# Attention and state-space kernel on one core: small loads reordered, an interleaving moved from GpSimd to VectorE, the last block's stores moved to SyncE, planner durations edited

## The chip, the cores and the metric

The kernel runs on one core of a Trainium2 chip. A core has five engines, each with its own instruction queue that is worked off in order: TensorE (PE in the profile; PEld are its weight loads), VectorE (DVE), ScalarE (ACT), GpSimd (POOL) and SyncE (SP). SP and ACT, and POOL in another way, also issue DMAs. The metric is device time in microseconds of one execution; it is compared as the median of several.

## The reference, cut to what matters

One sequence of 2048 rows and 448 columns goes through two branches that are mixed by a gate per row.

```
g = sigmoid((x * gate_w).sum(-1))
# A: 16 query heads of width 28, one shared key and value head
q = x @ wq;  k = x @ wk;  v = x @ wv
a = softmax(q k^T / sqrt(28)) v  @ wo
# B: a diagonal state-space model with 256 complex modes for each of 448 channels
dt = exp(log_dt);  K[d,l] = Re sum_n C[d,n] dt[d] B[d,n] exp(dt[d] A[d,n] l)
b = causal_convolution(K, x) + x * Dskip
out = g * a + (1 - g) * b
```

The scores are 16 heads x 2048 x 2048 exponentials. The convolution has one filter K of 2048 taps for every channel; the kernel makes the taps from tables of powers and convolves with matmuls on Toeplitz slices of the taps.

## The kernel before, in words

**Attention.** The scores are 1024 tiles of 128 keys by 512 queries (16 groups of a query chunk and four heads, 64 tiles each). TensorE makes a tile into one of five PSUM banks (lines 1289 and 1312, and 1300 and 1303 for the last 64 tiles), ScalarE exponentiates sets of three and two tiles in turn (line 1344, 410 instructions), and TensorE multiplies each with V (lines 1362 and 1356). Q of a later group is projected on TensorE (line 857), its absolute values and its copy are taken by VectorE (lines 863 and 869), and a copy in another layout, qM, is made by DMAs from POOL.

**Head.** Four x tiles are loaded by SP, transposed by TensorE (line 639), and copied by ScalarE (line 649) or VectorE (line 653) to xT. From them come K (line 661, copied by line 673), its maxima (line 668), V and the gate (line 684). The step sizes dt are spread over partitions by a matmul (line 768) and exponentiated by ScalarE (line 770). The raw parameters are transposed (line 781) and multiplied on VectorE (line 792); sines come from ScalarE (lines 798 and 799), whose table for the sine is loaded at a dummy instruction of one element (line 678) and whose table for the exponential is loaded again at another (line 800). Lines 804 and 807 are six more exponentials on 128x896, `tab` and five powers `mq`. K's and V's weights and `log_dt` are loaded by ACT's DMA queue, the rest by SP's.

**Convolution.** The channels are 14 blocks of 32. For each, VectorE builds the tables of powers (lines 896 to 916, 936 to 986; line 986 is the last of a block), TensorE multiplies them to taps (line 1009, 64 matmuls a block), VectorE copies the taps (line 1019), and POOL's DMAs write them to a scratch in device memory (KP_scratch). SP's DMAs load them back shifted, as slices T (some land in the buffer of U). Two convolutions of 16 channels each (128 matmuls each on line 1071, with x interleaved as U) follow, each with a product on VectorE (line 1080), a reversal by TensorE (line 1091) and an addition into O (line 1100). U is made from x rows in O by 16 copies on POOL (line 598) into U and T, and spread by SP's DMAs.

**End.** Three of four query chunks go through the output projection (line 1109) and are folded into O on VectorE (line 1118). The last chunk is normalised by matmuls (lines 1171 and 1178) and VectorE (1374, 1182, 1184), its four row tiles add O by a matmul with the identity (line 1209) and the projection (line 1205), and they are copied out by VectorE (line 1226) and ScalarE (line 1223). Large stores of O leave earlier.

**Order.** No order is written by hand. Each operation is recorded with its engine, a duration in ns, and a priority `pr`; `Prog.schedule` plays the program through with these durations, takes the ready operation with the earliest start and then the lowest `pr`, and writes every engine's list in that order. The chip then runs those lists, with semaphores for what depends. `LAZY` adds a delay to operations of certain priorities, and `pg.after` holds one operation behind another. A duration given to the planner changes no instruction, but it moves instructions in the lists. Where TensorE has a hole in the plan, the planner puts in a filler matmul (line 1271).

## Time and profile before

| | |
|---|---|
| median of 3 executions | 502.0 us (500.86, 502.0, 503.79) |
| the profiled execution | 503.36 us |
| its span, first to last instruction | 501.5 us |
| instructions | 17468 |
| granted TensorE clock, mean | 0.989 |
| first score exponential starts | 19.35 us |
| last score exponential ends | 494.73 us |

A profile row of a timeline gives the start, the length, the engine, the line of the kernel, the operation, what it writes and reads with shapes, the number of instructions merged in the row, and in brackets how long the engine had been idle before it and what ended that. Instructions on an engine overlap a little, so that the distance of two starts is shorter than a length. Windows give the busy time of each engine in a stretch, with the count of instructions. The chain of work that ended last is followed back from the last instruction, at each step to what released it.

### The profile page before, as it was taken

The numbers are of one execution on the slowest core, as the hardware profiler recorded it, in microseconds if no ns is written. First come the engines' busy times: TensorE is split into PE (matmuls) and PEld (weight loads), VectorE is DVE, ScalarE is ACT, GpSimd is POOL, SyncE is SP. The second block draws the span as 40 slices with busy tenths as digits, with TensorE's granted clock in tenths as the row PEclk, the third lists the DMA queues.
The fourth block names the chain that finished last, engine by engine and source line by source line (L and its number), as shares of the span: only waits on it lengthen the run. The fifth ranks groups of instructions, "written<-read, shape, count | busy, mean of one in ns | idle before, by whom it ended". The sixth has DMA issues, their size and how long they took to land.

```text
span 501.5 us, 17468 instructions
## 1 busy us (share of the span) xinstructions
PE 468.2 (93%) x7651; PEld 213.7 (43%) x7734; DVE 455.7 (91%) x862; ACT 485.0 (97%) x435; POOL 166.5 (33%) x308
## 2 busy tenths in 40 slices
PE   8899999999999999989999999988999999999997
PEld 6532233344443334444443434434444253455563
DVE  5999999999999999999999999989999999994222
ACT  5999999999999999999999999989999999999995
POOL 5106534233243243224316124521512540535110
PEclk9799999999999999999999999989999999999999
DMA  8997289847519348995934861799692666777942
GB/s 236 324 190 191 26 189 132 274 118 241 158 25 284 102 125 208 276 242 114 272 87 104 237 180 46 225 250 263 175 255 36 195 205 182 218 204 209 298 153 78
DMA packets 151527, 91.86 MB, mean 183 GB/s; under 512 B 83514, under 2 KB 147436, under 8 KB 151452
## 3 DMA queue, kind: packets, MB, share of 16 engines
q1 hardware_dynamic: 141962, 81.05, 60.2%
q0 software_dynamic: 8960, 9.54, 7.8%
q8 instruction: 60, 0.98, 0.8%
q10 hardware_dynamic: 530, 0.17, 0.2%
q14 instruction: 15, 0.12, 0.1%
HBM read 73.61 MB, written 5.23 MB: 157 GB/s over the span
## 4 chain that ended last, share of the span: by engine, by line
DVE 57%; ACT 23%; PE 16%; DMA 2%; issue 1%; SPq 0%
ACT expT L1344 22%; DVE tab L950 19%; DVE tab L965 10%; DVE tab L979 4%; DVE tmp L973 3%; DVE msq L896 3%; PE psS L1289 2%; DVE kstg L1019 2%; PE psB L1362 2%; PE psS L1312 2%; DVE cst L1080 2%; DMA T<-KP_scratch 1%; DVE seedz L898 1%; DVE mbf L916 1%; DVE acc L1127 1%; DVE qT L869 1%
## 5 line engine op out<-in xcount | busy, mean ns | idle before, releaser
L1344 ACT ACTIVATE expT<-psS 128x1536 bf16<-128x1536 f32 (+1 forms) x410 | 466.2, 1326 | 4.6 <-PE psS L1289 2.8
L950 DVE TENSOR_TENSOR tab<-tab,mbf 128x512 bf16<-128x512 bf16 (+4 forms) x140 | 140.4, 1007 | 0.0
L1289 PE MATMUL psS<-qT,kT 29*128 29x512 bf16 x654 | 92.2, 387 | 8.1 <-ACT expT L1344 4.0
L1362 PE MATMUL psB<-expT,vaug 128*32 128x512 bf16 x960 | 96.1, 391 | 0.4 <-DVE acc L1127 0.3
L151 POOL DMA_DIRECT2D KP_scratch<-kstg x112 | 61.6, 557 | 101.5 <-DVE kstg L1019 101.0
L1312 PE MATMUL psS<-qM,kT 128*128 128x512 bf16 x234 | 76.1, 383 | 11.8 <-issue 8.1
L965 DVE TENSOR_TENSOR tab<-tab 128x256 bf16<-128x256 bf16 (+4 forms) x140 | 78.6, 585 | 0.0
L1362 PEld LDWEIGHTS psB<-expT,vaug 128*32 128x32 bf16 x960 | 24.6, 93 | 70.6 <-issue 68.8
L1271 PE MATMUL psB<-ident,one 128*128 128x512 bf16 x168 | 53.9, 383 | 0.1
L151 POOL DMA_DIRECT2D qM<-qT x64 | 32.6, 515 | 58.5 <-DVE qT L869 37.2
L1289 PEld LDWEIGHTS psS<-qT,kT 29*128 29x128 bf16 x654 | 22.6, 91 | 55.9 <-ACT expT L1344 40.8
L151 POOL DMA_DIRECT2D rdenB<-R_scratch x60 | 30.3, 510 | 48.1 <-DMA R_scratch<-denT 48.0
L1071 PE MATMUL psS<-T,U 128*26 128x128 bf16 (+3 forms) x1792 | 40.0, 223 | 0.7 <-DMA T<-KP_scratch 0.7
L1071 PEld LDWEIGHTS psS<-T,U 128*26 128x26 bf16 (+3 forms) x1792 | 31.6, 106 | 15.0 <-issue 9.6
L1071 PE MATMUL psX<-T,U 128*32 128x128 bf16 (+3 forms) x1472 | 33.8, 222 | 1.5 <-issue 1.2
L979 DVE TENSOR_TENSOR tab<-tab,tmp 128x1984 bf16<-128x1984 bf16 x28 | 32.6, 1188 | 0.1
L1071 PEld LDWEIGHTS psX<-T,U 128*32 128x32 bf16 (+3 forms) x1472 | 25.4, 106 | 14.1 <-issue 10.9
L1312 PEld LDWEIGHTS psS<-qM,kT 128*128 128x128 bf16 x306 | 18.8, 97 | 26.6 <-ACT expT L1344 17.0
L973 DVE TENSOR_TENSOR tmp<-tmp,mq 128x64 bf16<-128x64 bf16 (+4 forms) x70 | 26.1, 373 | 0.2
L1271 PEld LDWEIGHTS psB<-ident,one 128*128 128x128 bf16 x168 | 15.2, 97 | 23.0 <-issue 13.1
L896 DVE TENSOR_TENSOR msq<-seedz 128x512 f32<-128x512 f32 (+1 forms) x40 | 24.9, 622 | 0.0
L151 POOL DMA_DIRECT2D R_scratch<-denT x15 | 8.5, 565 | 48.1 <-DVE denT L1133 20.1
(186 smaller groups left out, 522.3 us busy)
## 6 DMA issues: line engine op xcount, KB each, us to landing
T<-KP_scratch SPq DMA_DIRECT2D x204, 272.0 KB, 5.0
U<-KP_scratch SPq DMA_DIRECT2D x20, 272.0 KB
rdenB<-R_scratch POOLq DMA_DIRECT2D x60, 64.0 KB
U<-cst SPq DMA_DIRECT2D x1, 3584.0 KB, 23.8
qM<-qT POOLq DMA_DIRECT2D x64, 32.0 KB, 4.6
tab<-in_A_x_dram SPq DMA_DIRECT2D x4, 448.0 KB, 6.1
O<-in_A_x_dram SPq DMA_DIRECT2D x16, 112.0 KB, 2.9
O<-cst SPq DMA_DIRECT2D x1, 1792.0 KB, 10.6
```

The lines of the kernel that those rows point to most:

```text
L151: return [e.dma_start(o, i, **kw) for o, i in pairs]
L896: pg.op("dve", lambda e: e.tensor_tensor(m2(msq), z2, z2, ALU.mult), el(2 * n), rd=[kr, ki] + first, wr=["msq"], pr=pr)
L950: mul = lambda e, o, a, b: e.tensor_tensor(o, a, b, ALU.mult)
L965: vo(lambda e, dv=dv, tv=tv, k=k: e.tensor_tensor(dv, dv, tv, ALU.add if k else ALU.subtract), n, [kt[k], kd[k]], [kd[k]])
L973: vo(lambda e, w=w, lv=lv: e.tensor_tensor(rho.v(0, P, (32 - 2 * w) * 2, [[64, 32], [2, w], [1, 2]]), rho.v(0, P, (32 - w) * 2, [[64, 32], ...
L979: vo(lambda e, k=k: e.tensor_tensor(tab.v(0, P, FM + k * FP + 2, [[64, 32], [2, 31], [1, 2]]), tab.v(0, P, lm + k * PL + 62, [[64, 32], [- ...
L1071: r = e.matmul(ps.v(32 * j, 32 - m0, 128 * k, [[1, 128]]), self.U.v(0, P, (4 * gi + j) % UA // 2 * 128 + 2 * (2 * m0 + par) + j % 2, [[4, ...
L1271: return e.matmul(t.v(0, P, off, [[1, 512]]), self.one.v(0, P, 2, [[0, P]]), self.ident.v(0, P, 0, [[0, 4], [1, P]]), start=b != 6, stop=b ...
L1289: r = e.matmul(self.psS.v(0, P, 512 * b, [[1, 512]]), kT.v(32 * h, DH + 1, 128 * kt, [[1, 128]]), qT.v(32 * h, DH + 1, 512 * (i % 2), [[1, ...
L1312: return e.matmul(self.psS.v(0, P, 512 * b, [[1, 512]]), kT.v(0, P, 128 * kt, [[1, 128]]), self.qM.v(0, P, (i % 2) * XQ + 512 * h, [[1, 51 ...
L1344: pg.op("act", lambda e: e.activation(expT.v(0, P, 512 * es[0], spread(es, n)), self.psS.v(0, P, 512 * bs[0], spread(bs, n)), AF.Exp, scal ...
L1362: r = e.matmul(self.psB.v(32 * h, 32, 0, [[1, 512]]), vaug.v(0, P, 32 * kt, [[1, 32]]), expT.v(0, P, 512 * ring[t], [[1, 512]]), start=(kt ...
```

## The change

- `log_dt` is the first DMA on ACT's queue, ahead of K's weights. Its exponential and, right behind it, the sine's dummy (which loads the sine's table) come ahead of the first x copy on ScalarE; before, the dummy stood behind the third copy.
- The loads of V's weights and of the gate's weights move from ACT's queue to SP's, behind `wq` and ahead of the second raw parameter.
- The two memsets of qM move from POOL to VectorE.
- U is interleaved by four copies of 32-bit words on VectorE instead of 16 on POOL.
- The taps of block 13 are written to the scratch by SP instead of POOL.
- The warm-up matmuls write another PSUM bank.
- Priorities of the tap matmuls (1.4 to 1.15) and of the output projection (1.2 to 1.58), the table of delays that goes with them, and durations told to the planner are edited: the exponentials, the smallest table products and the fold into O. These change the order of the lists alone.

```diff
 GATE = (30, 35)
+XDVE = ((1, 0), (1, 1), (1, 2))
 WARM = 64
 NEWQ = 15
+LASTQ = 13
 STORES = (401, 405, 408)
...
     FAR = 2500.0
-    LAZY = {1.2: 200.0, 1.4: 200.0, 1.55: 200.0, 1.6: 200.0}
+    LAZY = {1.15: 200.0, 1.55: 200.0, 1.58: 200.0, 1.6: 200.0}
     LATE = 1000.0
...
         for k in range(2):
-            pm(V(self.qM, k * XQ, XQ), 0.0, 1800, [("qM", k)], 1.5)
+            dm(V(self.qM, k * XQ, XQ), 0.0, 1130, [("qM", k)], 0.5)
         self.identg = self.kstg.cast(F32)
...
         lx(0)
+        pg.dma([(self.dtb.v(0, 1, 0, [[1, D]]), dram(ins["B_log_dt"], 0, [[D, 1], [1, D]]))], (1, 896), "ldt", wr=["dt"], eng="act", extra=-1500)
         pg.dma([(wks.v(0, DT, 0, [[1, 112]]), dram(ins["A_wk"], 0, [[112, DT], [1, 112]]))], (112, 224), "wk", wr=["wks"], eng="act")
-        pg.dma([(self.dtb.v(0, 1, 0, [[1, D]]), dram(ins["B_log_dt"], 0, [[D, 1], [1, D]]))], (1, 896), "ldt", wr=["dt"], eng="act")
         lx(1)
-        pg.dma([(wks.v(0, DT, 112, [[1, 112]]), dram(ins["A_wv"], 0, [[112, DT], [1, 112]])),
-                (wks.v(0, DT, 224, [[1, 4]]), dram(ins["gate_w"], 0, [[4, DT], [1, 4]]))],
-               (224, 200), "wv", wr=["wvs"], eng="act", extra=1500)
         lx(2)
...
                (112, 3584), "wq", wr=["wqs"], fac=0.85)
+        pg.dma([(wks.v(0, DT, 112, [[1, 112]]), dram(ins["A_wv"], 0, [[112, DT], [1, 112]])),
+                (wks.v(0, DT, 224, [[1, 4]]), dram(ins["gate_w"], 0, [[4, DT], [1, 4]]))],
+               (224, 200), "wv", wr=["wvs"], extra=1500)
         lraw(1)
...
         pg.op("dve", lambda e: e.tensor_copy(self.Wv.v(0, DT, 0, [[32, 4], [1, DH]]), wks.v(0, DT, 112, [[DH, 4], [1, DH]])),
-              180, rd=["wvs"], wr=["Wv"], pr=0.1)
+              180, rd=["wvs"], wr=["Wv"], pr=0.3)
         pg.op("dve", lambda e: e.tensor_copy(self.Wv.v(0, DT, 28, [[32, 4]]), wks.v(0, DT, 224, [[1, 4]])),
-              100, rd=["wvs"], wr=["Wvg"], pr=0.1)
+              100, rd=["wvs"], wr=["Wvg"], pr=0.3)
         V0 = lambda b, off, n, r: b.v(0, P, off, [[n // r, r], [1, n // r]])
...
         done = []
+        U4, T4, O4 = (b.cast(mybir.dt.int32) for b in (self.U, self.T, self.O))
         for half in range(2):
             for k in range(2):
-                for j in range(0, 8, 2):
-                    jj = 8 * k + j
-                    if half == 0:
-                        dst, w = self.U.v(0, P, 2 * jj, [[128, UA // 2], [1, 4]]), ["Uz", ("Ub", k)]
-                    else:
-                        dst, w = self.T.v(0, P, UB + 2 * jj, [[32, UA // 2], [1, 4]]), ["rawdone", ("UB", k)]
-                    key = ("ustd", half, jj)
-                    done.append(key)
-                    pg.op("pool", lambda e, dst=dst, jj=jj, half=half: e.tensor_copy(
-                        dst, self.O.v(0, P, jj * D + half * UA, [[2, UA // 2], [D, 2], [1, 2]])), 660,
-                        rd=[("ust", k)] + ([] if half else []), wr=w + [key], pr=1 + half)
+                if half == 0:
+                    dst, w = U4.v(0, P, 8 * k, [[64, UA // 2], [1, 8]]), ["Uz", ("Ub", k)]
+                else:
+                    dst, w = T4.v(0, P, UB // 2 + 8 * k, [[16, UA // 2], [1, 8]]), ["rawdone", ("UB", k)]
+                key = ("ustd", half, k)
+                done.append(key)
+                pg.op("dve", lambda e, dst=dst, k=k, half=half: e.tensor_copy(
+                    dst, O4.v(0, P, (8 * k * D + half * UA) // 2, [[1, UA // 2], [D // 2, 8]])), 1000,
+                    rd=[("ust", k)] + ([] if half else []), wr=w + [key], pr=1 + half)
         for k, (c0, c1) in enumerate(((0, 2), (2, 5), (5, 9), (9, 14))):
...
         for i in range(18):
-            pg.op("pe", lambda e: e.matmul(self.psX.v(0, P, 0, [[1, 256]]), self.cst.v(0, P, 512, [[1, P]]), self.cst.v(0, P, 512, [[1, 256]]),
-                                           start=True, stop=True, tile_position=(0, 0)), 213, rd=[("cst", 1)], wr=["warm"], pr=3)
+            pg.op("pe", lambda e: e.matmul(self.psS.v(0, P, 4 * 512, [[1, 256]]), self.cst.v(0, P, 512, [[1, P]]), self.cst.v(0, P, 512, [[1, 256]]),
+                                           start=True, stop=True, tile_position=(0, 0)), 213, rd=[("cst", 1)], wr=["warm", ("b", 4)], pr=3)
         for q in range(4):
...
                 key = ("xT", hp, q)
-                if hp == 0 or q == 3:
-                    o = pg.op("act", lambda e, d=dst, s=src: e.activation(d, s, AF.Copy), 1000, rd=[("b", b)], wr=[key])
-                    if q == 0:
-                        self.xc0 = o.i
+                if (hp, q) not in XDVE:
+                    pg.op("act", lambda e, d=dst, s=src: e.activation(d, s, AF.Copy), 1000, rd=[("b", b)], wr=[key])
                 else:
...
                 km()
-            if q == 2:
-                pg.op("act", lambda e: e.activation(sm.v(0, P, 2, [[1, 1]]), sm.v(0, P, 1, [[1, 1]]), AF.Sin), 1340,
-                      rd=["hpi", ("xT", 0, 2)], wr=["dum"], pr=-3)
...
         o = pg.op("act", lambda e: e.activation(d1, pl(), AF.Exp), 500, rd=["ldx"], wr=["dt"], unlock=L)
-        pg.after[o.i] = self.xc0
+        d = pg.op("act", lambda e: e.activation(self.small.v(0, P, 2, [[1, 1]]), self.small.v(0, P, 1, [[1, 1]]), AF.Sin), 1340,
+                  rd=["hpi"], wr=["dum"], pr=-3)
+        pg.after[d.i] = o.i
         pg.op("dve", lambda e: e.tensor_scalar(dtp, d1, 1.0 / TWO_PI, None, ALU.mult), 300, rd=["dt"], wr=["rd"])
...
             pg.op("dve", lambda e: e.tensor_tensor(o, f(a), b, op), ns, rd=rd, wr=wr, pr=pr, **kw)
-        p0, k0 = trans(0, 0)
-        vt(tt(1), p0, dtp2, ALU.mult, [k0, "rd"], [K(1)], 0.2, unlock=p0)
+        p0, k0 = trans(0, -0.5)
+        vt(tt(1), p0, dtp2, ALU.mult, [k0, "rd"], [K(1)], -0.1, unlock=p0)
         pg.op("dve", lambda e: e.tensor_scalar(t(2), t(1), MAGIC, None, ALU.add), ns / 2, rd=[K(1)], wr=[K(2)], pr=-0.1)
...
                     e, A(do + k * PL, to + k * tw - do - k * PL), src, M(m, 128)),
-                   2 * n, done[0] + done[1][2:] + mk(lv), [kd[k], kt[k]] + late)
+                   2 * n, done[0] + done[1][2:] + mk(lv), [kd[k], kt[k]] + late, 1.92 if lv else 1.09)
             for k in range(2):
...
                 tv = tab.v(0, P, to + k * tw, [[64, 64], [1, 2 * w]])
-                vo(lambda e, dv=dv, tv=tv, k=k: e.tensor_tensor(dv, dv, tv, ALU.add if k else ALU.subtract), n, [kt[k], kd[k]], [kd[k]])
+                vo(lambda e, dv=dv, tv=tv, k=k: e.tensor_tensor(dv, dv, tv, ALU.add if k else ALU.subtract), n, [kt[k], kd[k]], [kd[k]], 1.92 if lv else 1.16)
             done = [done[0] + [kd[0]], done[1] + [kd[1]]]
...
                 pg.op("pe", mm, 245, mode="h", ni=16, rd=keys,
-                      wr=[(X, q), ("kst", q)], pr=1.4, lock=G if k == 0 else None)
+                      wr=[(X, q), ("kst", q)], pr=1.15, lock=G if k == 0 else None)
             o = 512 * q
...
                     ko.v(32 * g, 32, o + 64 * (g % 2), [[128, 4], [1, 64]])) for g in range(4)]
-            pg.dma(lst, (512, 128), f"kw{q}", rd=[("kst", q)], wr=[("KP", c, q)], pr=0, eng="pool", extra=1800)
+            if c < LASTQ:
+                pg.dma(lst, (512, 128), f"kw{q}", rd=[("kst", q)], wr=[("KP", c, q)], pr=0, eng="pool", extra=1800)
+            else:
+                pg.dma(lst, (512, 128), f"ks{q}", rd=[("kst", q)], wr=[("KP", c, q)], pr=0, iss=700.0)
...
                 start=(g == 0), stop=(g == 3), tile_position=(0, 0), skip_group_check=True), 200,
-                rd=["Wo"] + [("on", gg) for gg in range(4)], wr=[X], pr=1.2, lock=G if g == 0 else None)
+                rd=["Wo"] + [("on", gg) for gg in range(4)], wr=[X], pr=1.58, lock=G if g == 0 else None)
         self.fold(qc, tt, px, 0, D, [X], unlock=G)
...
         self.pg.op("dve", lambda e: e.scalar_tensor_tensor(ov, px(), self.gt.v(0, P, tl, [[1, 1]]), ov, ALU.mult, ALU.add),
-                   el(n), rd=rd + ["gt"], comm=(("O", tl), ("Oz", tl)), pr=2, unlock=unlock)
+                   el(n, 0.86), rd=rd + ["gt"], comm=(("O", tl), ("Oz", tl)), pr=2, unlock=unlock)
...
                                                 self.psS.v(0, P, 512 * bs[0], spread(bs, n)),
-                                                AF.Exp, scale=SQ), 58 + 512 * n / 1.2, rd=bk, wr=ew, pr=0)
+                                                AF.Exp, scale=SQ), 46 + 428 * n, rd=bk, wr=ew, pr=0)
```

More of the change, by code (lines that the diff above doesn't have):

```diff
@@ L664, in mk @@
                 return r
-            pg.op("pe", mk, 1100, rd=["Wk"] + self.xk(q), wr=[bk], lock=G)
+            o = pg.op("pe", mk, 1100, rd=["Wk"] + self.xk(q), wr=[bk], lock=G)
+            self.k3 = o.i
             kv = kT.v(0, P, 512 * q, [[1, 512]])
@@ L784, in mm @@
                 return r
-            pg.op("pe", mm, 700, rd=[("raw", k), "id"], wr=[X, "rawdone"], pr=pr, lock=t_)
+            self.rawx = pg.op("pe", mm, 700, rd=[("raw", k), "id"], wr=[X, "rawdone"], pr=pr, lock=t_).i
             return t_, X
```

## The prediction

> **What bounds the kernel now.** I read the page first, then the timeline of ScalarE (ACT), then the windows of the steady stretch, then VectorE's (DVE's) timeline, and last the tail. The page's first part, of the profiled execution:
>
> ```profile
> PE 468.2 (93%) x7651; PEld 213.7 (43%) x7734; DVE 455.7 (91%) x862; ACT 485.0 (97%) x435; POOL 166.5 (33%) x308
> ```
>
> ACT's 97% invites the reading "only ACT counts". The chain that ended last contradicts it:
>
> ```profile
> DVE 57%; ACT 23%; PE 16%; DMA 2%; issue 1%; SPq 0%
> ```
>
> What ACT needs at least is read from the starts of neighbouring rows of its timeline, where it never waits:
>
> ```profile
> 19.35 2.37 ACT L1344 ACTIVATE expT<-psS 128x1536 bf16<-128x1536 f32 x2 [0.16 <-PE psS L1289]
> ...
> 24.19 1.46 ACT L1344 ACTIVATE expT<-psS 128x1536 bf16<-128x1536 f32 x1
> 25.52 0.97 ACT L807 ACTIVATE mq<-T 128x896 bf16<-128x896 f32 x1
> 26.36 1.04 ACT L1344 ACTIVATE expT<-psS 128x1024 bf16<-128x1024 f32 x1
> 27.26 0.97 ACT L807 ACTIVATE mq<-T 128x896 bf16<-128x896 f32 x1
> ```
>
> A three-tile exponential takes 25.52 - 24.19 = 1.33 us from start to start, a two-tile one 27.26 - 26.36 = 0.90: five score tiles in 2.235 us, 0.4475 us a tile, 458.2 us for all 1024. The first starts at 19.35, the last (a row "473.61 21.12 ... x19") ends at 494.73. Six other instructions, L804 and the five of L807, lie in between (0.84 each from start to start; with L708, 5.1 us). So 494.73 - 19.35 - 5.1 - 458.2 = 12.1 us are stalls of ACT, nearly all too short to be rows. Who causes them? In the windows VectorE has no idle time (columns: window, length, then PE, PEld, DVE, ACT, POOL busy):
>
> ```profile
> 60.00:300.00 240.00, 226.67 (x3572) 97.83 (x3614) 239.66 (x438) 238.65 (x212) 78.83 (x146) 1.00 0.68 175
> 300.00:345.00 45.00, 40.50 (x772) 18.92 (x781) 42.92 (x85) 42.17 (x38) 14.94 (x28) 0.96 0.71 196
> 345.00:455.00 110.00, 103.92 (x1943) 48.50 (x1963) 108.19 (x199) 109.86 (x98) 38.63 (x71) 1.00 0.69 190
> 455.00:495.00 40.00, 38.88 (x917) 21.96 (x919) 10.44 (x20) 39.73 (x36) 8.59 (x16) 1.00 0.65 196
> ```
>
> DVE is full until 455 and idle after. The tables of a channel block end with L986; block 13's is
>
> ```profile
> 453.39 0.69 DVE L986 TENSOR_SCALAR tab<-tab 128x2048 bf16<-128x2048 bf16 x1
> ```
>
> TensorE works in order, and in its built order the tap matmuls of block 13 (L1009) stand after 938 of the 1024 score tiles. ACT at its own pace from 19.35 + 5.1 = 24.45 would need them at 24.45 + 938 x 0.4475 = 444.2; the tables end at 454.1, 9.9 us late. The same sum for blocks 1, 5, 9 and 11 (tiles 180, 443, 700, 828; L986 ends 105.6, 224.6, 343.9, 403.6) gives 0.6, 1.9, 6.2 and 8.7. So VectorE falls behind the written order, steadily, and ACT's stalls are that lateness handed on. After 454.1 ACT runs almost free: 86 tiles x 0.4475 = 38.5, and 494.73 - 454.1 - 38.5 = 2.1 us of stalls.
>
> **The change, part by part.**
>
> *The order of TensorE.* This is the large part: new durations in the planner move work between the score tiles. Counted in the two built orders, block 13's tap matmuls stand after 955 tiles instead of 938, blocks 9 to 12 after 715, 793, 845, 903 instead of 700, 780, 828, 883; the first nine blocks move by 5 tiles at most. Behind VectorE's last tables there are then 69 tiles: 69 x 0.4475 + 2.1 = 33.0 us instead of 40.6, so 7.6 us less if the tables end when they did. The other end pays: the last convolution ended after tile 1010, now its last matmuls stand behind the last score tile.
>
> *VectorE's load until 454.1.* Its instructions up to block 13's tables are the same set but for six. The two qM memsets (1024 words; the row of 128 words takes 0.17, so about 1.1 each) fall into its waits of 1.87 us before L495 and 1.95 before L549: nothing, or 1.1 each without them. Four interleaving copies of 896 words are added, bounded by L795 on 128x896 f32 (0.54 from start to start) and L796 (1.0): 2.1 to 4.0 us; I take 4.0, as strided words have no faster row. POOL's sixteen copies (43.4 to 56.3 us) go, and with them this, shown on one line:
>
> ```profile
> 42.13 0.29 DVE L900 TENSOR_TENSOR seedz<-msq 128x128 f32<-128x128 f32 x1
> ...
> 43.81 0.59 DVE L900 TENSOR_TENSOR seedz<-msq 128x128 f32<-128x128 f32 x1
> ...
> 46.17 0.66 DVE L900 TENSOR_TENSOR seedz<-msq 128x128 f32<-128x128 f32 x1
> ```
>
> While POOL copies, equal instructions take twice as long: four of L900 and four of L916 lose 0.33 each, three of L898 0.25, three larger ones 0.8 together: 4.2 us given back. Ahead of qT's first copy, which opens the dense stretch, stand two more products (L791, 1.0 each) that came later before; walked by hand that copy ends at 21.05 instead of 18.76: 2.3 - 2.0 = 0.3 lost. Last, DVE waited 45 - 42.92 + 110 - 108.19 = 3.9 us between 300 and 455, mostly for TensorE. The new order could take that to 0 or double it; the two other executions were 1.4 and 2.5 us shorter, so I take 1.4 off. Together 4.0 - 4.2 + 0.3 - 1.4 = -1.3: tables at 452.8.
>
> *Head.* The step sizes lead ACT's DMA queue; they landed at 5.47 behind the K weights and need about 4.5 now (x's first tile, issued at the same 0.82, began to land at 4.3). TensorE's product stands behind 15 of 18 warm-up matmuls (1.14 + 15 x 0.21), so the exponential (0.42) starts at 4.8, the sine's load and dummy (10.66 to 12.06, 1.4) end at 6.7, and the first x copy starts 0.45 late (6.24); the second is on time, and the 1.4 us that stood ahead of the second kT copy are gone. L803 and three of L806 then run ahead of the first score exponential, at 21.75, with 1.75 us of such work left: ACT's own start 23.5 instead of 24.45. Since VectorE sets the end this counts for nothing; without that cover it is 0.95. Two DMA issues leave ACT (0.33 and 0.44) in a wait that lasts until 6.24: nothing. On SP they stand behind wq and ahead of five parameter loads, whose landing (13.3 for the next) was set by transfers, not issues; 25 KB more is under 0.3. V's weights land near 12.9 instead of 8.9, and their copy stands on DVE behind work until 15.2: hidden by 2.3 us; later than that, DVE's queue and all of K's maxima behind it wait.
>
> The Trainium skill, ScalarE: Activation LUTs, What ACT_TABLE_LOAD costs, gives 1.28 us for the load and 1.38 for a drain at each switch. Here L678's load takes 1.28 and its dummy starts 0.02 later, so no drain is seen; by the page the first x copy would start 1.4 us later still, and with all of it handed on the sum would be 499.2; I give that 0.03, counted inside the forecast's chance.
>
> *Last taps.* Eight issues go from POOL (0.56) to SP (0.62 for a tap load). SP's tap loads for convolution 26 wait behind the second four. From the last tap matmul (tile 968): copy 0.7, four issues 2.5, four loads 2.5, landing 5.0: 10.7 us, 24 tiles; TensorE needs them at 995. Hidden by 1.4 us. The interleaved U is ready near 51 instead of 56.3: nothing waits for it that early.
>
> *Tail.* Before, the end came 501.5 - 494.73 = 6.8 us after the last exponential. Now behind it on TensorE stand three fillers, the last convolution's reversal (0.45) and, behind DVE's fold of it, all four output tiles, 20 matmuls at 0.19. With the rows of before (acc copy 0.4, L1171, L1182, L1178: ready at +2.85; 20 x 0.19 to +6.65; ACT's copy to the end 501.5 - 498.5 = 3.0) it is 9.75, with the fillers 0.65 in the way 10.4. I take 10.1: 3.3 us lost.
>
> *Sum.* 452.8 + 33.0 = 485.8 for the last exponential (ACT's own pace would allow 23.5 + 458.2 = 481.7, so VectorE still sets it), + 10.1 = 495.9; the run's time stood 503.36 - 501.5 = 1.86 over its span: 497.8. That is 5.6 below the profiled execution and 4.2 below the median of 502.0.
>
> **The rivals.**
> 1. The lateness isn't VectorE's to shed: TensorE's many short waits make it, so DVE only looks full, ACT's stalls stay at 12.1, and the longer tail is all that shows: 503.36 - 0.95 + 3.3 = 505.7. For it: TensorE is busy 39 of 40 us too. Against: VectorE's idle time of 0.34 us in 60 to 300. It is slower than now by over 0.5% once the last exponential ends after 492.5.
> 2. The interleaving copies wait on DVE: they need the loads that landed at 43.31 and 48.39, and DVE reaches them at 45.8 and 48.9. A second load 3 us later stops DVE for 2.5: 500.3; with the 3.9 us of waits kept as well 501.7.
> 3. Late last taps: SP's small writes may land like its other writes to that scratch (8.8 us) instead of POOL's 2.3: TensorE stands about 2 us, and the clock follows. At 327.1 a wait of 0.72 us was followed by half clock until 333.4 and 0.92 + 0.95 us of lost ACT time in the windows 325 to 335: 501 in all, with the wait itself.
> 4. The half clock of the head (20 to 25 us, granted 0.50) meets score exponentials instead of the parameter work now moved ahead: 1.9 us, 499.7.
>
> **How the numbers follow.** Chances: forecast 0.57, rivals 0.14, 0.13, 0.09, 0.07. About 0.5%, 2.5 us, is what a measurement of this kernel can tell from no change: faster is below 499.5, slower above 504.5. The forecast's own range: copies at 2.1 and no waits reach ACT's own limit, 481.7 + 1.7 + 9.75 + 1.86 = 495.0; waits kept and the long tail 499.5. Rivals 2 to 4 end within, rival 1 slower; a tenth of the forecast spills over: faster 0.57, same 0.31, slower 0.12. Low 495.0, high 503.5.
>
> **What would show it.** Last exponential near 486 and end 10 us behind it; L1008 of block 13 starting less than 4 us behind 23.5 + 955 x 0.4475 = 450.9; no doubled L899 rows at 44 to 56; the four copies near 1.0 each; first score exponential at 21 to 22.5. Wrong: tables of block 13 after 457, or ACT's stalls still above 10 us.

## The result and the profile after

The changed kernel takes 505.94 us (median of 12, 504.35 to 509.33), the kernel before 502.35 (median of 12, 500.86 to 503.95): ratio 1.0072, 95% interval 1.0052 to 1.0092. It is slower by 3.6 us; 497.8 was forecast, with 0.12 for this side. The profiled execution took 504.67 (span 502.9), 1.3 more than the one of before: that one lies 1.0 above its kernel's median and this one 1.3 below, so the two traces show 1.4 of the 3.6 us.

The page's first part after the change, and the chain that ended last:

```profile
PE 476.6 (95%) x7722; PEld 211.7 (42%) x7722; DVE 457.1 (91%) x868; ACT 483.9 (96%) x435; POOL 145.6 (29%) x282
...
ACT 88%; PE 9%; DVE 2%; issue 1%
```

VectorE was 57% of the chain and is 2%. The windows of the same stretches (window, length, then PE, PEld, DVE, ACT, POOL busy, clock, DMA share, GB/s):

```profile
60.00:300.00 240.00, 232.50 (x3633) 97.57 (x3632) 238.35 (x441) 239.76 (x213) 79.80 (x148) 1.00 0.68 175
300.00:345.00 45.00, 43.72 (x850) 19.84 (x850) 44.55 (x80) 45.00 (x41) 14.09 (x27) 1.00 0.75 207
345.00:455.00 110.00, 105.75 (x1836) 46.50 (x1838) 108.92 (x201) 110.00 (x99) 38.84 (x72) 1.00 0.68 184
455.00:495.00 40.00, 36.95 (x953) 22.07 (x952) 9.40 (x19) 35.82 (x32) 3.24 (x6) 1.00 0.63 183
```

Until 455 ACT has hardly any idle time in these windows (most stalls told below are too short for them); behind that it is busy 35.8 of 40 us. VectorE's timeline at block 13's tables:

```profile
454.06 0.68 DVE L985 TENSOR_SCALAR tab<-tab 128x2048 bf16<-128x2048 bf16 x1
...
460.02 0.69 DVE L1018 CAST kstg<-psS 128x512 bf16<-128x512 f32 x1 [2.94 <-PE psS L1008]
```

The tables end at 454.7 (454.1 before), but TensorE comes to block 13's taps only at 458.1; now VectorE waits. The same holds for every block: TensorE's first tap matmul starts 0.7 to 4.1 us behind the tables. Before, it started within 0.1 us of them in blocks 0, 1, 2, 7 and 12 alone; in the other nine it came 0.2 to 4.6 us behind tables that were ready.

To see where the time went I take the starts of the 15th and the 381st of the 410 score exponentials, the end of the last, and the span's end:

| | 15th | 381st | last ends | span ends |
|---|---|---|---|---|
| before | 40.83 | 461.11 | 494.73 | 501.5 |
| after | 42.59 | 457.17 | 493.29 | 502.9 |

So the head costs 1.8, the middle gives 5.7 back (414.6 us instead of 420.3; without a stall these 366 exponentials take 183 x (1.331 + 0.904) = 409.0), the stretch from the 381st on costs 2.5, the tail 2.9. Sum: +1.4, as the spans say.

Not all of the middle's gain is the new order's. Before, 2.5 us of ACT's stalls lie between 325 and 335, where TensorE waited for a tap load and its granted clock was half from 330.0 to 333.4; after, 0.1 lie there. Apart from this stretch the middle gives back 3.3.

```profile
327.83 0.48 PE L1071 MATMUL psS<-T,U 128*32 128x128 bf16 x20 [0.72 <-DMA T<-KP_scratch]
```

The head's loss, on ACT's timeline:

```profile
27.91 1.02 ACT L1346 ACTIVATE expT<-psS 128x1024 bf16<-128x1024 f32 x1
29.58 1.45 ACT L1346 ACTIVATE expT<-psS 128x1536 bf16<-128x1536 f32 x1 [0.65 <-PE psS L1291]
31.24 1.02 ACT L1346 ACTIVATE expT<-psS 128x1024 bf16<-128x1024 f32 x1 [0.21 <-PE psS L1291]
33.07 2.37 ACT L1346 ACTIVATE expT<-psS 128x1536 bf16<-128x1536 f32 x2 [0.81 <-PE psS L1314]
```

Before, powers of the parameters stood between these exponentials; three of them now run ahead of the first. From the first score exponential to the 15th ACT's own pace takes 7 x 2.235 = 15.65 us, and parameter work 5.1 before and 1.7 now. Of 40.83 - 19.35 and of 42.59 - 22.09 that leaves 0.7 us of stalls before and 3.1 after: ACT's own start (the first one's, plus the parameter work still to come) is 0.6 earlier, and the stalls are 2.4 more. They are waits for TensorE. Two of TensorE's own waits for VectorE stand ahead of them:

```profile
20.44 0.39 PE L865 MATMUL psX<-qT,Wb 128*128 128x512 bf16 x1 [1.62 <-DVE Wb L695]
...
24.15 0.93 PE L780 MATMUL psS<-ident,T 112*128 112x112 bf16 x8 [1.08 <-DVE tab L791]
```

The windows (columns as above), before and then after:

```profile
20.00:22.50 2.50, 2.50 (x26) 1.72 (x23) 2.46 (x3) 2.50 (x4) 1.31 (x3) 0.50 1.12 343
22.50:25.00 2.50, 2.50 (x14) 1.25 (x14) 2.44 (x8) 2.50 (x5) 0.27 (x1) 0.50 1.15 305
```

```profile
20.00:22.50 2.50, 1.87 (x27) 1.17 (x28) 2.02 (x5) 2.50 (x4) 0.64 (x1) 0.94 1.12 334
22.50:25.00 2.50, 1.42 (x15) 1.02 (x12) 2.50 (x4) 2.50 (x4) 1.50 (x4) 0.50 1.13 305
```

From 25 to 35 us TensorE then has no idle time (10.0 of 10 us). I read the stalls as this lost time coming late; no run isolates it. The half clock alone isn't the cause: before had 6.8 us of it too (19.4 to 26.2; now 22.2 to 29.0), and the waits that end at 31.24 and 33.07 come with the clock at full. The late loss, ACT first, then TensorE:

```profile
483.31 5.97 ACT L1346 ACTIVATE expT<-psS 128x1536 bf16<-128x1536 f32 x5 [1.18 <-PE psS L1302]
490.15 1.02 ACT L1346 ACTIVATE expT<-psS 128x1024 bf16<-128x1024 f32 x1 [0.86 <-PE psS L1305]
```

```profile
482.63 0.30 PE L1073 MATMUL psX<-T,U 128*26 128x128 bf16 x8 [1.54 <-issue]
...
488.86 0.39 PE L1358 MATMUL psB<-expT,vaug 128*32 128x256 bf16 x6 [1.17 <-issue]
```

"Issue" means that TensorE waited for nothing that the profile shows. The page's part on DMA queues names one for instructions:

```profile
q8 instruction: 60, 0.98, 0.8%
```

Its 60 packets hold 16 KB each. These two waits start 256 instructions of TensorE apart, and each ends 1.2 to 1.3 us behind a packet that moved from 480.26 to 481.40 and from 486.38 to 487.53. TensorE's next instructions came late.

### The profile page after: what moved, and what is told of

It is laid out like the page before. It is cut to its first block, busy times and chain, and to the rows that moved or that the text cites. A ratio compares the mean times of both kernels' runs of the same rounds, so it can differ in the third digit from the quotient of the medians.

```text
span 502.9 us, 17507 instructions
## 1 busy us (share of the span) xinstructions
PE 476.6 (95%) x7722; PEld 211.7 (42%) x7722; DVE 457.1 (91%) x868; ACT 483.9 (96%) x435; POOL 145.6 (29%) x282
## 4 chain that ended last, share of the span: by engine, by line
ACT 88%; PE 9%; DVE 2%; issue 1%
ACT expT L1346 86%; PE psB L1358 1%; PE psB L1267 1%; PE psS L1305 1%; PE psS L630 1%; PE psX L1073 1%; PE psS L1291 1%; PE psS L1314 1%; PE psS L1302 0%; PE psB L1273 0%; PE psS L1073 0%; PE psB L1364 0%; PE psX L1207 0%; PE psS L1207 0%; ACT L803 0%
## 5 line engine op out<-in xcount | busy, mean ns | idle before, releaser
L1291 PE MATMUL psS<-qT,kT 29*128 29x512 bf16 x654 | 91.5, 386 | 12.1 <-ACT expT L1346 7.4
L1314 PE MATMUL psS<-qM,kT 128*128 128x512 bf16 x306 | 92.1, 384 | 1.5 <-ACT expT L1346 1.1
L153 POOL DMA_DIRECT2D KP_scratch<-kstg x104 | 56.9, 554 | 72.8 <-DVE kstg L1018 68.8
L1273 PE MATMUL psB<-ident,one 128*128 128x512 bf16 x152 | 48.8, 384 | 0.0
L1073 PE MATMUL psX<-T,U 128*26 128x128 bf16 (+3 forms) x1920 | 44.3, 221 | 2.3 <-issue 2.1
L1073 PEld LDWEIGHTS psX<-T,U 128*26 128x26 bf16 (+3 forms) x1920 | 33.2, 106 | 18.6 <-issue 12.5
L153 POOL DMA_DIRECT2D denT<-acc x15 | 11.1, 740 | 102.2 <-DVE acc L1129 89.6
L1073 PE MATMUL psS<-T,U 128*32 128x128 bf16 (+3 forms) x1344 | 30.1, 221 | 0.0
L1314 PEld LDWEIGHTS psS<-qM,kT 128*128 128x128 bf16 x306 | 18.3, 97 | 27.7 <-ACT expT L1346 18.8
L1073 PEld LDWEIGHTS psS<-T,U 128*32 128x32 bf16 (+3 forms) x1344 | 23.1, 105 | 10.0 <-issue 7.4
L1008 PE MATMUL psS<-tab 128*64 128x128 bf16 x608 | 26.1, 223 | 0.0
```

Of the source, the lines that this page charges most:

```text
L153: return [e.dma_start(o, i, **kw) for o, i in pairs]
L1008: r = e.matmul(G.v(64 * u, 64, 128 * k, [[1, 128]]), tab.v(0, P, lo + comp * PL + cg * 64 + u, [[2, 64]]), tab.v(0, P, fo, [[64, 2], [mo - ...
L1073: r = e.matmul(ps.v(32 * j, 32 - m0, 128 * k, [[1, 128]]), self.U.v(0, P, (4 * gi + j) % UA // 2 * 128 + 2 * (2 * m0 + par) + j % 2, [[4, ...
L1273: return e.matmul(t.v(0, P, off, [[1, 512]]), self.one.v(0, P, 2, [[0, P]]), self.ident.v(0, P, 0, [[0, 4], [1, P]]), start=b != 6, stop=b ...
L1291: r = e.matmul(self.psS.v(0, P, 512 * b, [[1, 512]]), kT.v(32 * h, DH + 1, 128 * kt, [[1, 128]]), qT.v(32 * h, DH + 1, 512 * (i % 2), [[1, ...
L1314: return e.matmul(self.psS.v(0, P, 512 * b, [[1, 512]]), kT.v(0, P, 128 * kt, [[1, 128]]), self.qM.v(0, P, (i % 2) * XQ + 512 * h, [[1, 51 ...
```

## The experiments

Any edit makes the planner write all lists anew, so a run differs from its neighbour in more than the edit, except where the lists are said to keep their order. All ratios are to the kernel before in the same job; the times on the right are of one profiled execution. Such an execution can hold a stretch of half clock that others of its kernel lack: in the middle before (330.0), e2 (260.2), e4 (265.1), e6 (233.5 to 240.3) and e14 (59.8), in the late stretch e7, e9, e10, e12 and e15.

| run | median us | ratio, 95% interval | 15th | 381st | last | end |
|---|---|---|---|---|---|---|
| e1 less VectorE, before | 498.98 | 0.9933, 0.9906 to 0.9959 | 41.28 | 456.52 | 490.51 | 497.3 |
| e2 planner's edits alone | 505.91 | 1.0081, 1.0050 to 1.0112 | 40.21 | 456.81 | 494.22 | 503.8 |
| e3 head alone | 504.95 | 1.0058, 1.0027 to 1.0088 | 42.63 | 460.83 | 495.13 | 502.1 |
| e4 change, old planner values | 505.23 | 1.0053, 1.0022 to 1.0084 | 42.99 | 461.45 | 496.71 | 503.5 |
| e5 change, short loads | 504.26 | 1.0040, 1.0014 to 1.0065 | 42.75 | 457.85 | 491.43 | 501.1 |
| e6 change, L803 held | 508.56 | 1.0134, 1.0088 to 1.0180 | 42.10 | 459.71 | 496.07 | 505.5 |
| e7 exponential's duration alone | 504.40 | 1.0042, 1.0013 to 1.0071 | 40.46 | 458.69 | 496.06 | 503.4 |
| e8 less VectorE, change | 507.07 | 1.0088, 1.0056 to 1.0121 | 43.64 | 459.92 | 496.32 | 506.0 |
| e9 change, no head fillers | 505.68 | 1.0075, 1.0051 to 1.0098 | 43.15 | 457.87 | 495.65 | 505.2 |
| e10 change, old head | 505.29 | 1.0056, 1.0031 to 1.0082 | 41.80 | 457.42 | 496.26 | 504.8 |
| e11 change, late stores | 507.35 | 1.0105, 1.0076 to 1.0135 | 42.95 | 460.25 | 496.70 | 506.3 |
| e12 old head, lean | 507.45 | 1.0114, 1.0075 to 1.0153 | 43.69 | 462.17 | 500.04 | 509.1 |
| e13 head, no priorities | 508.27 | 1.0099, 1.0068 to 1.0130 | 42.42 | 460.90 | 495.67 | 502.4 |
| e14 loads alone | 505.59 | 1.0049, 1.0016 to 1.0081 | 42.63 | 462.59 | 496.69 | 503.5 |
| e15 change, no priorities | 508.34 | 1.0102, 1.0063 to 1.0140 | 42.36 | 458.81 | 496.24 | 504.9 |
| e16 change, held stores | 506.75 | 1.0072, 1.0043 to 1.0102 | 43.17 | 460.21 | 495.37 | 505.0 |

### Does VectorE set the end? (e1, e8)

```diff
+            rows = 32 if c == 0 else 8
-            vo(lambda e, k=k: e.tensor_tensor(tab.v(0, P, FM + k * FP + 2, [[64, 32], [2, 31], [1, 2]]),
+            vo(lambda e, k=k, rows=rows: e.tensor_tensor(tab.v(0, P, FM + k * FP + 2, [[64, rows], [2, 31], [1, 2]]),
...
```

> The kernel before, with VectorE's two products that fill each block's outer table (128x1984, 1.19 us each) cut to a quarter of their rows in blocks 1 to 13: that part of the taps is left out, and the planner is told the old durations, so that every list keeps its order. About 13 x 2 x 0.85 = 22 us of VectorE's work go, spread evenly. Theory A (the prediction's: VectorE is late against the written order and ScalarE's stalls are that lateness handed on): the last exponential falls from 494.7 to ScalarE's own limit, 24.45 + 458.2 + 2.1 = 484.8, the time by about 10 to 492.5. Theory B (the stalls are made by TensorE's own waits at a few places, and VectorE's lateness is mostly taken up elsewhere): less than 4 us, 498.5 to 502.

> The changed kernel with VectorE's two outer products cut to a quarter of their rows in blocks 1 to 13 (that part of the taps is left out), order kept: about 22 us of VectorE's work less. In the changed kernel TensorE comes to each block's taps 0.7 to 4.1 us after the tables are there, so Theory B says that VectorE no longer sets anything: 0 to 1.5 us faster, 504.4 to 506. Theory A (VectorE still sets the end by its copies and products elsewhere): 5 us or more, below 501.

The page of e1, first part and chain:

```profile
PE 479.0 (96%) x7734; PEld 213.2 (43%) x7734; DVE 438.0 (88%) x862; ACT 483.4 (97%) x435; POOL 166.5 (33%) x308
...
ACT 83%; PE 7%; DVE 5%; DMA 3%; SPq 1%; issue 1%
```

VectorE lost 17.7 us of busy time, and the kernel before became 3.4 us faster by its ratio, not 10; 15th to 381st exponential takes 415.2 us, still 6.2 above the floor. That is theory B. In the changed kernel the same cut (438.2 us of DVE) gains nothing (1.0088 against 1.0072, intervals that overlap), and block 13's tables end no earlier (456.6): VectorE follows there. So VectorE's lateness was worth at most 5 of the 11.3 us of stalls in the middle, and 1.6 of these 5 lie between 325 and 335, where e1's execution has no half clock; its ratio says 3.4. The rest is not VectorE's own. The new order sheds about as much (5.7, or 3.3 without that stretch).

### The parts alone (e2, e3, e4, e7, e10)

```diff
-    LAZY = {1.2: 200.0, 1.4: 200.0, 1.55: 200.0, 1.6: 200.0}
+    LAZY = {1.15: 200.0, 1.55: 200.0, 1.58: 200.0, 1.6: 200.0}
...
-                                                AF.Exp, scale=SQ), 58 + 512 * n / 1.2, rd=bk, wr=ew, pr=0)
+                                                AF.Exp, scale=SQ), 46 + 428 * n, rd=bk, wr=ew, pr=0)
```

e2 is this with the change's other priorities and durations, on the kernel before; e4 is the change without them; e7 is the last pair of lines alone.

> The kernel before with the planner's edits alone (priorities, delays, durations): block 13's tap matmuls stand after 960 score tiles instead of 938, and the tail is the long one. Theory A: the last exponential at 454.1 + 64 x 0.4475 + 2.1 = 484.8, the end 10 behind it, 496.7 in time, 5.7 faster. Theory B: the long tail (+2.85) and the stalls of 2.8 us that the last convolution makes at 480 to 492 come, less what the middle sheds (0 to 5.9): 502 to 508.

> The changed kernel with the planner's edits undone: block 13's tap matmuls again after 938 tiles, 13 of the last 20 matmuls of the output behind the last score tile, as before. Theory A: tables at 454.7 and 86 tiles behind them: last exponential 495.3, end 6.8 behind it, 504.0 in time, about 2 faster than the changed kernel and 1.6 slower than before. Theory B: head stalls stay (+1.6 against before), the stalls at 480 to 492 and the long tail go (-5.65 against the changed kernel), what the middle does is open: 500 to 504; if the middle keeps the changed kernel's 5.65 us of stalls, 500.

> The kernel before with one planner edit alone, the duration of the score exponentials: block 13's tap matmuls stand after 946 score tiles instead of 938 and only the 20 output matmuls behind the last score tile, no convolution. Theory B and C: the middle sheds 2 to 4 us of stalls as in the run of the planner's edits alone, the dense end stays out, the tail is 1.3 longer: 499 to 502. If the middle's gain depends on the other edits, 503 to 504.

```diff
         lx(0)
+        pg.dma([(self.dtb.v(0, 1, 0, [[1, D]]), ...)], (1, 896), "ldt", wr=["dt"], eng="act", extra=-1500)
...
-        p0, k0 = trans(0, 0)
+        p0, k0 = trans(0, -0.5)
```

e3 is the head's edits on the kernel before, e10 the change without them.

> The kernel before with the edits of the head alone (order of the small loads, the exponential of the step sizes and the sine's table ahead of the first x copy, V's weights on SP, warm-up bank, two priorities). Theory A: VectorE sets the end, its dense stretch opens 0.3 us later: 502.6. Theory B: ScalarE's stalls of 2.2 us between 25 and 42 us come back whole, less 0.6 of earlier own start: +1.6, 504.

> The changed kernel with the head's edits undone, all others kept: block 13's tap matmuls after 950 tiles, the last convolution's matmuls ahead of the last score tile, its 16 reversals and the 20 output matmuls behind it. The fifteenth score exponential started 1.76 us later in the changed kernel than before (42.59, 40.83). If parts add up: 505.9 - 1.8 = 504.1, less up to 1 for the shorter tail, with the stalls past 475 us kept. If the head's loss was taken back later by slack, 505 to 506.

The planner's edits alone cost 4.1 us by the ratio (theory B; theory A had them 5.7 faster). Their middle is 3.7 us shorter than before (416.6), but 381st to last takes 37.4 instead of 33.6 and the tail 9.6 instead of 6.8. The head alone costs 2.9, with the 15th exponential at 42.63. e4 against e3 (505.23, 504.95) leaves the interleaving on VectorE and the last taps on SP at nothing that can be told. The parts don't add up: 4.1 and 2.9 alone, 3.6 together; undoing the head under the new plan brings the 15th exponential 0.8 back, and the 381st starts where it did (457.42, 457.17). e7 has the short list behind the last score tile and loses the late stretch all the same (37.4). Its trace has TensorE's wait of the same kind as the two above, with half clock from 486.5 to 489.9 behind it:

```profile
486.02 0.39 PE L1300 MATMUL psS<-qT,kT 29*128 29x256 bf16 x5 [1.65 <-issue]
```

No single edit was found that keeps the gain.

### The late stretch (e5, e11, e16)

```diff
         for h in range(4):
-            to = bass.AP(tensor=buf.h, offset=h * rs + o, ap=[[4 * rs, 32], [TC, 8], [1, TC]])
+            nr = 8 if gi < 52 else 1
+            to = bass.AP(tensor=buf.h, offset=h * rs + o, ap=[[4 * rs, 32], [TC, nr], [1, TC]])
...
```

> The changed kernel with the last block's four tap loads (channels 416 to 447) cut to an eighth of their bytes: the taps of seven eighths of those channels are left out of the convolution; every list keeps its order and its count of instructions. Theory C (the stalls at 480 to 492 are TensorE waiting for its own instructions, whose fetch queues behind the tap loads on the DMA engines): the fetches of 480.26 and 486.38 start about 1 us behind the block's start instead of 4, the idle times of 1.5 and 1.2 us named issue go, ScalarE's stalls past 480 fall from 2.8 to below 1, the time falls by 2 to 3 us from 505.9. Theory D (256 instructions of TensorE are simply too few for so dense a stretch, whatever the DMAs do): stalls and time stay.

Windows of the changed kernel, then of e5 (columns as above):

```profile
470.00:480.00 10.00, 9.86 (x256) 6.16 (x253) 2.16 (x5) 10.00 (x10) 1.98 (x4) 1.00 1.00 300
480.00:488.00 8.00, 6.14 (x147) 3.58 (x148) 1.71 (x3) 6.82 (x7) 0.00 (x0) 1.00 1.04 333
```

```profile
470.00:480.00 10.00, 9.86 (x242) 5.96 (x240) 2.17 (x5) 10.00 (x10) 1.97 (x4) 1.00 0.32 75
480.00:488.00 8.00, 7.77 (x190) 4.74 (x187) 1.71 (x3) 8.00 (x8) 0.00 (x0) 1.00 0.55 173
```

With DMA share 0.32 instead of 1.00, TensorE is busy 7.77 of 8 us instead of 6.14, ACT 8.00 instead of 6.82, no wait for instructions is left, and stalls past 475 fall from 2.9 to 0.2. Theory C on the waits. Its 2 to 3 us of time show in the trace (the last exponential 1.9 earlier) but less in the medians: 1.0040 against 1.0072, 1.6 us, with intervals that overlap. The kernel before had its full DMA queues at 470 to 480 (1.08) and empty ones at 480 to 488 (0.26): its tap loads left 4.4 us earlier, ahead of the dense matmuls.

```diff
-STORES = (401, 405, 408)
+STORES = (407, 408, 409)
```

> The changed kernel with the three large stores of O held behind score exponentials 407, 408 and 409 instead of 401, 405 and 408; TensorE's list is the same. Theory C: the second late wait of TensorE for its instructions (487.4, fetch started at 486.38 while the stores of 479 filled the DMA engines) goes, the first (480.82, behind the tap loads) stays: stalls past 475 us 1.5 instead of 2.9, time 504.3 to 505 unless the end then waits for the stores. Theory D (density alone): both waits stay.

This tested nothing: the hold orders the lists only, and on the chip the stores left at 483.53, right behind the last load. e16 holds them by a dependency:

```diff
-                       (512, 832), f"out{qc}", rd=[("O", 4 * qc + k) for k in range(4)], pr=1)
+                       (512, 832), f"out{qc}", rd=[("O", 4 * qc + k) for k in range(4)] + [("acc", 1, 1)], pr=1)
```

> The changed kernel with the three large stores of O held by a dependency on the copy behind the last score tiles (1.25 MB, so about 4 us of transfer behind 494); TensorE's list is the same. Theory C: the first late wait for instructions, behind the tap loads, stays (near 480.8), the second (487.4) goes since the DMA engines are empty by then; stalls past 475 us 1.5 to 1.8 instead of 2.9; time 504.5 to 505 unless the end waits for the stores. Theory D (density alone): both stay, 506.

SP's queue and windows of e16:

```profile
479.80 2.93 SPq L153 DMA_DIRECT2D U<-KP_scratch  x4
496.40 5.88 SPq L153 DMA_DIRECT2D out_dram<-O  x7
```

```profile
484.00:488.00 4.00, 2.90 (x86) 1.77 (x88) 0.25 (x1) 3.26 (x3) 0.00 (x0) 1.00 1.05 350
488.00:492.00 4.00, 4.00 (x99) 2.29 (x88) 1.29 (x2) 4.00 (x5) 0.00 (x0) 1.00 0.05 15
```

Past 475 one wait for instructions is left (1.10, while the loads run at 1.05), the second is gone with the traffic (0.05); stalls past 475 are 1.05. The mechanism is as theory C said. The time isn't: 506.75, no less than the changed kernel's by the ratio (1.0072 both), and in its profiled execution TensorE waited 2.0 us for a tap load at 215.1 and 1.0 at 343.3, which the changed kernel's didn't.

### The head (e6, e9, e13, e14, e15, e12)

```diff
+            if s == HOLD:
+                pg.after[self.k5] = pg.ops[-1].i
```

> The changed kernel with one exponential of the parameters (L803) held behind the first score exponential, which moves VectorE's product that waits for it (L791 at 19.03) behind qT's copy. Theory E (the head's stalls come from that product: it delays Wb, so TensorE idles 1.62 us, falls to half clock and makes score tiles too slowly): qT's copy about 1.4 us earlier, TensorE's wait below 0.7 us, first score exponential before 21.3, ScalarE's stalls before 42 us 1.2 or less instead of 2.6, time 504 to 504.9. Theory F (ScalarE merely has less parameter work left to fill the half-clock stretch with, and the clock falls whatever stands on VectorE): stalls stay above 2, 505.5 to 506.5.

q's copy came 1.4 us earlier (19.46) as theory E said, TensorE's wait fell from 1.62 to 0.90, the first score exponential to 21.19. Yet 2.7 of the 3.1 us of stalls up to the 15th exponential stayed, though the half clock was down to 3.4 us (25.2 to 28.7), and the middle got worse (417.6, with half clock from 233.5 to 240.3 in it). Theory F as to the size of the stalls; its cause, the half clock, doesn't fit.

```diff
-            if s < WARM and ts[0] % 64 < 52 and (ts[0] < 64 or ts[0] % 64 > 14):
+            if 9 <= s < WARM and ts[0] % 64 < 52 and (ts[0] < 64 or ts[0] % 64 > 14):
...
-            if e == "pe" and (opened or spare) and r > self.FWIN and self.filler is not None and npe > self.FIRST + self.BLOCK:
+            if e == "pe" and (opened or spare) and r > 36000.0 and self.filler is not None and npe > self.FIRST + self.BLOCK:
```

> The changed kernel without filler and warming matmuls (L1267, L1273) in the first 36 us; they stood between the score tiles there, 3.4 us of TensorE's time between 26 and 34. In that stretch TensorE has no idle time and ScalarE waits for it. Theory G (TensorE's own load in the head is what makes ScalarE wait, and the fillers are part of that load): ScalarE's stalls before 42 us fall from 2.6 to 1 or less, the fifteenth score exponential starts near 41 instead of 42.59, the time falls by 1 to 2 us. Theory H (the clock sets it, and without fillers it stays at half): stalls stay above 2.5, and the time is the changed kernel's 505.9 or more.

> The changed kernel with the old head, without fillers in the first 36 us and with the late stores. If the theories C and G hold and parts add up: -1.8 (head) - 1.4 (second fetch) - 0.5 (shorter list behind the last score tile) from 505.9: 502.2; below 500 only if the middle, 5.7 us better in the changed kernel than before, keeps that too and the first fetch wait goes by chance.

Without fillers the half clock lasted longer (0.50 granted until 32.5; with them 0.70 at 27.5 to 30), the stalls up to the 15th exponential were 2.6 and that one no earlier (43.15): what the fillers' absence gave, the clock took, as I read it. e12, the change with the old head, without these fillers and with the late stores, was expected at 502.2. It is slower than the kernel before, and no faster than the changed one.

```diff
-        p0, k0 = trans(0, -0.5)
-        vt(tt(1), p0, dtp2, ALU.mult, [k0, "rd"], [K(1)], -0.1, unlock=p0)
+        p0, k0 = trans(0, 0)
+        vt(tt(1), p0, dtp2, ALU.mult, [k0, "rd"], [K(1)], 0.2, unlock=p0)
```

This on e3 is e13, on the change e15; e14 is the order of the small loads and the warm-up bank alone (with the two priorities of the copies of V's and the gate's weights), on the kernel before.

> The kernel before with the head's edits but without the two priorities of the first raw parameter (its transposes and its product keep 0 and 0.2). TensorE's list then has the projection of q ahead of the fourth K matmuls again. Theory P (the priorities make the head's loss: the product on VectorE ahead of q's copy, and the projection of q 3 us later): q's copy ends near 19.5 instead of 21.5, first score exponential near 20 instead of 22.3, fifteenth near 41 instead of 42.6, time 502 to 503.5 against 504.95 with them. Theory L (the loads and the table order make it): 504.5 to 505.5.

> The changed kernel without the same two priorities; block 13's tap matmuls after 953 tiles, the last convolution's matmuls ahead of the last score tile. Theory P with parts that add up: -1.6 (head) - 0.8 (shorter list at the end): 503.5. If what the head gains is lost again later, as in the run with the old head, 505 to 506.

> The kernel before with the order of the small loads and the warm-up bank alone. Theory P: within 0.7 of before, 501.8 to 503, fifteenth score exponential at 40.8 plus or minus 0.7. Theory L: 503.5 or more.

Theory P falls on the 15th exponential: without the priorities it still starts at 42.4. The first does come earlier, as P said (20.61 in e13, 22.29 in e3), and the stalls between them shrink from 3.0 to 1.1. But all 5.1 us of parameter work then stand between the two, and ACT's own start is 25.7 instead of 24.0. e14 shows that the loads' new order is enough for as late a 15th exponential (42.63), by that same way: 0.5 us of stalls, own start 26.5. Three rows of e14, from the timelines of VectorE, ACT and TensorE:

```profile
12.68 0.63 DVE L551 COPY Wq<-mbf 112x1792 bf16<-112x1792 bf16 x1 [1.43 <-DMA mbf<-in_A_wq_dram]
```

```profile
17.27 0.95 ACT L798 ACTIVATE T<-T 128x896 f32<-128x896 f32 x1 [2.45 <-DVE T L796]
```

```profile
19.62 0.42 PE L684 MATMUL psB<-expT 112*128 112x29 bf16 x8 [2.16 <-DVE Wb L698]
```

The planner now puts the copy of Wq ahead of the first product on VectorE; it waits 1.43 us for its load, everything behind it is late, and half clock begins during TensorE's wait of 2.16 (18.8 to 25.7, as long as before). What it doesn't explain: e13 and e15 have medians near 508.3, and e13's profiled execution is the fastest of its ten (504.26, at a mean clock of 0.992; the others had 0.982 to 0.990), so no trace shows what the slower ones lost.

In ten of the sixteen runs (e3, e4, e6, e7, e8, e11, e12, e13, e15, e16) the median lies above every time that was written ahead. The traces show where stalls sit in single executions; they don't account for these medians.

## Why the prediction was wrong, point by point

- **The order of TensorE, and the claim under it.** This is the step that failed: "VectorE falls behind the written order, steadily, and ACT's stalls are that lateness handed on", with "7.6 us less". The counting was right (955 tiles), the tables came at 454.7 (452.8 said), and VectorE's lateness did vanish. But block 13's taps started at 458.1 instead of 450.9, and the trace of before had the sign of it: of the blocks that I summed as ever later, TensorE came to blocks 5, 9 and 11 by 0.98, 2.49 and 0.21 us behind tables that were ready. I took ACT's own pace as the next limit, as if TensorE had no stalls of its own: 5.6 us of stalls between the 15th and the 381st exponential stayed, and e1 leaves 6.2 with 17.7 us of VectorE's work gone. Full windows of VectorE said that it was busy, not that it was what ACT waited for; of the 12.1 us, at most 5 were its own, 3.4 by e1's ratio.
- **The stretch behind the last tables.** "69 x 0.4475 + 2.1" moved work towards the end and costed nothing for it; 35.2 us passed from block 13's first tap matmul to the last exponential. Nor were the 2.1 us stalls: before, 0.3 were lost past 460, and at 454.1 ACT had started 935 tiles, not 938. The later taps put their loads beside the densest matmuls, the instruction fetches waited behind them, and stalls past 475 rose from 0.3 to 2.9. No rival had this.
- **The head.** First score exponential 22.09 (21.75 said), first x copy 0.76 late (0.45). That an earlier own start of ACT is worth up to 0.95 was wrong in sign: 1.8 lost by the 15th exponential. ACT's own start did come 0.6 earlier, and its stalls rose by 2.4. Rival 4 had 1.9 us for half clock that meets score exponentials; it met them, but e6 keeps most of the stalls with half as much of it, so that the cause of the head's loss stays open in part. It is no alternative to the forecast but a cost that came besides.
- **VectorE's load.** Four copies of 0.95 to 0.97 (4.0 said, 3.8 measured), one wait of 0.21, so rival 2 fell; L899 at 44 to 50 us takes 0.30 instead of 0.6, as said. These readings held and were worth nothing, since VectorE no longer sets the end. Its tables came 1.9 later than said all the same; the 1.4 us taken off for waits rested on two of three other executions, and the third (503.79) was longer than the profiled one.
- **Last taps.** No wait of the last convolutions for their taps shows, so rival 3 fell.
- **Tail.** 9.6 us, 10.1 said: right, as was what stands in it.
- **The table load.** The sine's load ran from 5.60 to 6.88 and its dummy started at 6.89, the x copy at 7.00. No drain of 1.38 us is there; the page of the Trainium skill, ScalarE: Activation LUTs, What ACT_TABLE_LOAD costs, is borne out for the load (1.28) only.
- **Sum.** 485.8 was said for the last exponential, 493.3 measured: 1.9 for the tables, 3.4 for TensorE's coming behind them, 2.2 for the stretch after. The longer tail then decides the sign. Rival 1 gave 505.7 for that case, and its point of decision (492.5) was passed. Its picture, stalls that stay as they were, was half right: by the prediction's own sum 11.3 us (493.29 - 22.09 - 1.7 - 458.2) instead of 12.1 in all, but in other places, 2.4 more in the head and 2.6 past 475, less in the middle. That its 505.7 lies 0.2 from the median is luck.

## What to carry to other kernels

A full engine at the end of the chain may be a follower: before costing a reordering by its lateness, ask what the next engine waits for without it, and give that engine's own stalls a price (here 5 to 6 us in 415). When work moves towards the end, count what goes with it: its loads, and the instructions of a dense stretch, which come over the same DMA engines. An edit of planner values rewrites every list, so its parts can't be added up.

## What the runs showed of the hardware

- TensorE's instructions come in packets of 16 KB, 256 instructions each (60 packets for 15,508 instructions in the trace of after). Counted in blocks of 256 from the late waits back, the median packet of the changed kernel started 0.54 us behind a block's start where the DMA engines were less than 60% busy in the 2 us from that start (27 blocks, 1.24 at most) and 2.4 where they were busier (33 blocks); ahead of the two late waits it was 4.1 and 3.8. All 38 waits of TensorE over 0.5 us named issue past 30 us, in 15 of the 18 traces, end 1.2 to 1.6 us behind the end of such a packet; e1, e5 and e14 have none. The Trainium skill, DMA: Bandwidth & Descriptors, Queues, rings and completion order, has each DMA engine take turns between its queues packet by packet; the runs agree in so far as the fetches are late only beside full queues.
- Half clock came in stretches of 3.4, 6.8 and 10.2 us (13.7 in e9's head, 17.1 in e12's), around or behind single waits of TensorE of 0.7 to 2.2 us, with work on both sides of them. Not each such wait brought it: none followed that of 1.54 at 482.63.
- Executions of the changed kernel go with their mean granted clock: of the twelve, six at 0.993 average 505.2 us, three at 0.990 505.7, those at 0.989, 0.987 and 0.983 took 506.6, 508.2 and 509.3. It isn't so in every run: e6 has 509.58 at 0.993 and 506.91 at 0.990.
